# Array tiles for the query side of a sketched-attention kernel: four 32-row tiles, 64x64 tiles, and x^T without transposes

## The chip, the cores and the metric

One core of one Trainium2 chip. The metric is the device time of one execution in microseconds (us), median of several. The profile is a recording of one execution; its span runs from the first to the last instruction. In the executions that were both recorded and timed, the time is about 1.8 us longer than the span (338.94 against 337.1, 340.63 against 338.8), so I compare times with times and spans with spans. The recorded execution of the kernel before (span 363.5) is none of those timed: by the same 1.8 us it took about 365.3 us.

Engines in the profile: PE is TensorE (matmuls), PEld its weight loads, DVE is VectorE, ACT is ScalarE, POOL is GpSimd, SP is SyncE. L272 is line 272 of the file of the kernel before; the lines shift between kernels.

## The reference

Two blocks in a row, in float32:

```python
# q, k, v: [4, 4, 1088, 32]; S1, S2: [8, 32]
def phi(x):
    a = np.einsum('rd,bhsd->bhsr', S1, x)
    b = np.einsum('rd,bhsd->bhsr', S2, x)
    return np.einsum('bhsi,bhsj->bhsij', a, b).reshape(*x.shape[:-1], 64)
q_p, k_p = phi(q), phi(k)
kv = np.einsum('bhsf,bhsd->bhfd', k_p, v)
z = np.sum(k_p, axis=2)
num = np.einsum('bhsf,bhfd->bhsd', q_p, kv)
den = np.einsum('bhsf,bhf->bhs', q_p, z)[..., None] + 1e-06
x = (num / den)            # heads side by side: [4352, 128]
h = x @ w_in               # [128, 2048]
g = 0.5 * h * (1.0 + erf(h / sqrt(2)))
out = g @ w_out            # [2048, 128]
```

S1, S2, w_in and w_out arrive as float64 and are rounded to float32 on the chip. That rounding works on the bits and is done by VectorE, in eight instructions for each of eight weight quarters.

## The kernel before

The tokens are cut into nine chunks: eight of 512 tokens and a remainder of 256. For each chunk the MLP runs 16 steps of one hidden matmul (w_in, then gelu on ScalarE) and one output matmul (w_out), and the attention work for the next chunk is woven between the steps. `bufs` counts the PSUM banks (8 together, in both kernels): three for hidden, one for output, three "work" banks, one for keys.

```python
    hps = ctx.enter_context(tc.tile_pool(name="hps", bufs=3, space=PSUM))
    ops = ctx.enter_context(tc.tile_pool(name="ops", bufs=1, space=PSUM))
    wps = ctx.enter_context(tc.tile_pool(name="wps", bufs=3, space=PSUM))
    kvps = ctx.enter_context(tc.tile_pool(name="kvps", bufs=1, space=PSUM))
# ... cut: loads, constants, keys ...
        def expand(i, hp):           # factor i (0: S1, 1: S2) of one half of the rows
            rows = slice(hp * 64, hp * 64 + 64)
            ps = work_bank()
            nc.tensor.matmul(ps[:, :W], lhsT=Srep[i][rows].rearrange("p g f -> p (g f)"),
                             rhs=T["qT"][rows, :W], start=True, stop=True)
            if i == 0:
                T["A", hp] = att.tile([128, CW], FP, name="A_sb")
                nc.scalar.copy(out=T["A", hp][:, :W], in_=ps[:, :W])
            else:
                T["qp", hp] = att.tile([128, CW], FP, name="q_pT")
                nc.vector.tensor_mul(out=T["qp", hp][:, :W], in0=T["A", hp][:, :W], in1=ps[:, :W])

        def num_over_den(hp):        # tokens on partitions; 33 columns a head: numerator and denominator
            ps = work_bank()
            for i in range(nt):
                for (r0, r1, b) in owners[i]:
                    nc.tensor.matmul(ps[r0:r1, i * 2 * C:(i + 1) * 2 * C],
                                     lhsT=T["qp", hp][:, i * 128 + r0:i * 128 + r1],
                                     rhs=kv_of(b, i, hp), start=True, stop=True)
            # ... cut: views ...
            nc.vector.tensor_scalar(out=den[:, :2 * nt], in0=nd[:, :, D], scalar1=1e-6, scalar2=None, op0=AX.add)
            nc.vector.reciprocal(out=den[:, :2 * nt], in_=den[:, :2 * nt])
            nc.vector.tensor_mul(out=x_of(T["x"], hp), ...)   # cut: operands

        def x_transposes():          # back to [channel, token]
            ps = work_bank()
            for i in range(nt):
                nc.tensor.transpose(ps[:, i * 128:(i + 1) * 128], in_=T["x"][:, i, :], identity=ident)
            xT[n] = att.tile([128, CW], FP, name="xT")
            nc.vector.tensor_copy(out=xT[n][:, :W], in_=ps[:, :W])
# ... cut: the MLP; the woven stages are spread evenly over the 15 first steps:
            for f in woven[fi * len(woven) // (NF - 1):(fi + 1) * len(woven) // (NF - 1)]:
                f()
```

Of the kernel before, what the change touches and what calls it, by code (L numbers as in the profile page):

```python
# [8 lines left out]
FP = mybir.dt.float32  # L9
# [7 lines left out]
def kernel(  # L17
# [11 lines left out]
    """Sketched attention into x^T, chunk by chunk, then gelu(x @ w_in) @ w_out on each chunk.  # L29

    Tokens of a batch lie as (p j): partition p holds J tokens in a row. The last REM tokens of each batch
    are kept apart, those of two batches in one tile. All arithmetic is float32; inputs that come as float64
    come as raw bits and are rounded to float32 on chip.
    """
# [23 lines left out]
    hps = ctx.enter_context(tc.tile_pool(name="hps", bufs=3, space=PSUM))  # L58
    ops = ctx.enter_context(tc.tile_pool(name="ops", bufs=1, space=PSUM))
    wps = ctx.enter_context(tc.tile_pool(name="wps", bufs=3, space=PSUM))  # L60
# [25 lines left out]
    def landing(dst, wide):  # L86
        """Where a parameter is loaded to: its own tile, or one of 64-bit words that is rounded into it."""
        if wide:
            raw[dst.name] = big.tile([dst.shape[0], dst.shape[1], 2], U32, name=f"raw_{dst.name}")
            return raw[dst.name].rearrange("p n two -> p (n two)")  # L90
        return dst

    def words(a):
        """A parameter in DRAM in 4-byte elements, and how many of them make one number."""
# [12 lines left out]
    def round_bits(dst):  # L107
        """float64 bits to the nearest float32: mantissa as an integer times a power of two with the sign."""
# [11 lines left out]
        # exponents from 2^-127 (nought) to 2^128 (infinity)  # L120
# [24 lines left out]
    ident = big.tile([128, 128], FP, name="ident")  # L145
    mask4 = big.tile([128, H], FP, name="mask4")
    mask2 = big.tile([128, 2], FP, name="mask2")
    kv_dup = [big.tile([128, H, 2 * C], FP, name=f"kv_dup{b}") for b in range(B)]
    kv_pair = [big.tile([128, NP, 2 * C], FP, name=f"kv_pair{b}") for b in range(B)]
    make_identity(nc, ident)  # L150
    nc.gpsimd.memset(mask4, 0.0)
    nc.gpsimd.memset(mask2, 0.0)
    for h in range(H):
        nc.gpsimd.memset(mask4[h * D:(h + 1) * D, h:h + 1], 1.0)
        nc.gpsimd.memset(mask2[h * D:(h + 1) * D, h % 2:h % 2 + 1], 1.0)
    for t in kv_dup + kv_pair:
        nc.gpsimd.memset(t, 0.0)
# [3 lines left out]
    wide = [big.tile([128, R, R], FP, name=f"wide{i}") for i in range(2)]  # L161
    Srep = [big.tile([128, 2, F], FP, name=f"Srep{i}") for i in range(2)]
# [6 lines left out]
    for i in range(2):  # L169
        src = sT[:, 0:R, None] if i == 0 else sT[:, None, R:2 * R]  # L170
        nc.vector.tensor_copy(out=wide[i], in_=src.broadcast_to([128, R, R]))
        nc.vector.tensor_mul(out=Srep[i],
                             in0=wide[i].rearrange("p i j -> p (i j)")[:, None, :].broadcast_to([128, 2, F]),
                             in1=mask2[:, :, None].broadcast_to([128, 2, F]))

# [4 lines left out]
    def key_stages(b):  # L180
# [18 lines left out]
        def features(n, pair=None):  # L199
# [11 lines left out]
            for i in range(n):  # L211
                # group i is head i with its groups over j, or else the one group over the heads
# [22 lines left out]
        def finish():  # L235
# [3 lines left out]
            for j in range(2):  # L239
                src = kv3[j * F:(j + 1) * F, :, j * C:(j + 1) * C]  # L240
                for i in range(2):
                    nc.vector.tensor_copy(out=kv_dup[b][i * F:(i + 1) * F, j::2, i * C:(i + 1) * C], in_=src)  # L242
                nc.vector.tensor_copy(out=kv_pair[b][j * F:(j + 1) * F, :, j * C:(j + 1) * C], in_=src)
# [11 lines left out]
    xT = {}  # L255

    def query_stages(n, srcs, owners, kv_of, x_of):
# [170 lines left out]
```

## Time and profile before

| | before |
|---|---|
| time, median | 363.39 us (363.19 to 364.63, the first 3 runs) |
| span of the profile | 363.5 us |
| TensorE, VectorE, ScalarE busy | 95%, 29%, 26% of the span |
| first hidden matmul of chunk 0 | 37.4 us |
| a full chunk without keys, with keys | 35.7, about 43 us |

The profile is read in three steps, which the prediction shows with its lines: the page's first parts tell which engine fills the span; stretches cut at each chunk's first hidden matmul tell in which stage that holds; and in TensorE's timeline the distance between the starts of neighbours prices one inserted piece. Matmul ends are modelled and overlap (an MLP line in the timeline of the kernel before lasts 1.02 us and its like starts 0.86 us after it), so durations of TensorE lines are not added up. One float32 matmul of 512 columns is two records there (the passes): 256 lie under the 128 output matmuls of the full chunks.

### The profile page before, as it was taken

The page shows a single profiled execution, that of the slowest core. Times are in us where ns is not written, and L with a number is a line of the kernel's source. Part 1 is how long each engine was busy: PE and PEld are TensorE (multiplying, and loading weights), DVE is VectorE, ACT ScalarE, POOL GpSimd, SP SyncE. Part 2 cuts the span into 40 slices and gives each one's busy share as a digit, 9 for nine tenths or more (in the row PEclk, how much of TensorE's full clock was granted, in tenths as well). Part 3 has the DMA queues.
Part 4 walks back from the last instruction along what each step waited for, and adds up shares of the span by engine and source line. Part 5 has one row for each costly group of instructions (what it writes and reads, how often), then busy time and mean ns, then how long its engine had stood idle before and what let it go on. Part 6 is the DMA issues. An engine that isn't in the chain of part 4 may idle for free.

```text
span 363.5 us, 3051 instructions
## 1 busy us (share of the span) xinstructions
PE 345.7 (95%) x1141; PEld 178.2 (49%) x1141; DVE 103.9 (29%) x254; ACT 96.1 (26%) x173; POOL 8.4 (2%) x34
## 2 busy tenths in 40 slices
PE   1888999999999999999999999999999999999993
PEld 0875456354345663453355653543454345444582
DVE  3357796922011422230112230320122011101100
ACT  1001221323323223133223213233223322332331
POOL 4002001000000000000000000000000000000000
PEclk9999999999999999999999999999999999999997
DMA  5999100000000000000000000000000000000000
GB/s 146 327 361 348 21 0 0 2 0 29 1 2 0 29 0 2 1 0 29 0 2 0 29 0 2 0 30 0 2 0 29 0 0 2 29 0 0 0 32 14
DMA packets 13854, 13.31 MB, mean 37 GB/s; under 512 B 3856, under 2 KB 12304, under 8 KB 13840
## 3 DMA queue, kind: packets, MB, share of 16 engines
q1 hardware_dynamic: 13840, 13.13, 11.2%
q8 instruction: 9, 0.15, 0.2%
q14 instruction: 5, 0.04, 0.0%
HBM read 10.90 MB, written 2.23 MB: 36 GB/s over the span
## 4 chain that ended last, share of the span: by engine, by line
PE 92%; DVE 4%; DMA 1%; issue 1%; SPq 0%; ACT 0%; DVEq 0%
PE o_ps L343 34%; PE h_ps L334 32%; PE w_ps L272 8%; PE kv_ps L225 6%; PE w_ps L285 4%; PE w_ps L202 3%; PE w_ps L354 1%; PE w_ps L301 1%; PE w_ps L265 1%; DMA raw_SR<-in_S_dram 1%; PE w_ps L195 1%; DVE kv_dup L242 0%; DVE bits_m L118 0%; DVE k_p L213 0%; DVE bits_e L121 0%
## 5 line engine op out<-in xcount | busy, mean ns | idle before, releaser
L343 PE MATMUL o_ps<-g,w_out 128*128 128x512 f32 (+1 forms) x288 | 144.2, 585 | 0.4 <-DVE w_out L124 0.4
L334 PE MATMUL h_ps<-xT,w_in 128*128 128x512 f32 (+1 forms) x288 | 142.3, 579 | 0.6 <-DVE xT L303 0.6
L337 ACT ACTIVATE g<-h_ps 128x512 f32<-128x512 f32 (+1 forms) x144 | 82.6, 574 | 220.1 <-PE h_ps L334 220.1
L334 PEld LDWEIGHTS h_ps<-xT,w_in 128*128 128x128 f32 x288 | 54.2, 193 | 59.0 <-issue 56.5
L343 PEld LDWEIGHTS o_ps<-g,w_out 128*128 128x128 f32 x288 | 48.3, 190 | 43.9 <-issue 23.1
L279 DVE TENSOR_TENSOR q_pT<-A_sb,w_ps 128x512 f32<-128x512 f32 (+1 forms) x18 | 11.8, 658 | 95.1 <-PE w_ps L272 81.0
L272 PE MATMUL w_ps<-qT,Srep 64*128 64x512 f32 (+1 forms) x72 | 37.7, 668 | 0.0
L225 PEld LDWEIGHTS kv_ps<-v_aug,k_p 128*128 128x128 f32 x128 | 19.7, 226 | 8.0 <-issue 5.8
L272 PEld LDWEIGHTS w_ps<-qT,Srep 64*128 64x128 f32 x72 | 10.9, 200 | 24.8 <-issue 21.2
L285 PEld LDWEIGHTS w_ps<-kv_dup,q_pT 128*128 128x128 f32 x128 | 18.2, 209 | 8.7 <-issue 8.0
L225 PE MATMUL kv_ps<-v_aug,k_p 128*128 128x66 f32 x128 | 19.8, 307 | 1.3 <-DVE k_p L213 1.3
L285 PE MATMUL w_ps<-kv_dup,q_pT 128*128 128x66 f32 x128 | 17.7, 288 | 0.5 <-DVE q_pT L279 0.5
L292 DVE TENSOR_SCALAR den<-w_ps 128x8 f32<-128x8 f32 (+1 forms) x18 | 3.0, 166 | 48.6 <-PE w_ps L285 48.6
L213 DVE TENSOR_TENSOR k_p<-a_t,w_ps 128x256 f32<-128x256 f32 x32 | 11.3, 415 | 13.0 <-ACT a_t L206 13.0
L276 ACT COPY A_sb<-w_ps 128x512 f32<-128x512 f32 (+1 forms) x18 | 9.9, 563 | 12.4 <-PE w_ps L272 12.4
L267 DVE COPY qT<-w_ps 128x512 f32<-128x512 f32 (+1 forms) x9 | 6.0, 662 | 24.0 <-PE w_ps L265 23.9
L202 PEld LDWEIGHTS w_ps<-S,kT 128*128 128x128 f32 x68 | 10.6, 228 | 4.4 <-DVE kT L197 2.5
L202 PE MATMUL w_ps<-S,kT 128*128 128x64 f32 x68 | 11.0, 310 | 1.4 <-DVE kT L197 1.4
L197 DVE COPY kT<-w_ps 128x512 f32<-128x512 f32 (+1 forms) x10 | 6.1, 608 | 21.6 <-PE w_ps L195 21.6
L347 DVE COPY o_sb<-o_ps 128x512 f32<-128x512 f32 (+1 forms) x9 | 6.0, 662 | 17.6 <-PE o_ps L343 17.6
L206 ACT COPY a_t<-w_ps 128x128 f32<-128x128 f32 (+1 forms) x10 | 2.5, 249 | 27.2 <-PE w_ps L202 27.2
L303 DVE COPY xT<-w_ps 128x512 f32<-128x512 f32 (+1 forms) x9 | 6.0, 662 | 8.6 <-PE w_ps L301 8.6
(63 smaller groups left out, 121.4 us busy)
## 6 DMA issues: line engine op xcount, KB each, us to landing
k<-in_k_dram SPq DMA_DIRECT2D x4, 512.0 KB, 9.3
v<-in_v_dram SPq DMA_DIRECT2D x4, 512.0 KB, 9.7
q<-in_q_dram SPq DMA_DIRECT2D x4, 512.0 KB, 9.7
raw_w_in<-in_moe_w_in_dram SPq DMA_DIRECT2D x4, 512.0 KB, 7.2
raw_w_out<-in_moe_w_out_dram SPq DMA_DIRECT2D x4, 512.0 KB, 8.2
out_dram<-oT SPq DMA_DIRECT2D x8, 256.0 KB, 2.0
k_rem<-in_k_dram SPq DMA_DIRECT2D x4, 32.0 KB, 4.1
v_rem<-in_v_dram SPq DMA_DIRECT2D x4, 32.0 KB, 2.6
```

The source lines that it names most:

```text
L197: nc.vector.tensor_copy(out=T["kT"][:, :n * 128], in_=ps[:, :n * 128])
L202: nc.tensor.matmul(ps[:, i * 64:(i + 1) * 64], lhsT=T["kT"][:, i * 128:(i + 1) * 128], rhs=S12.rearrange("p h r -> p (h r)"), start=True, ...
L213: nc.vector.tensor_mul(out=k_p[:, :, i] if pair is None else k_p[:, 0], in0=a[:, i * H:(i + 1) * H, :, None].broadcast_to([128, H, R, R]), ...
L225: nc.tensor.matmul(T["kv"][:, hp * 2 * C:(hp + 1) * 2 * C], lhsT=lhs[:, hp * 128:(hp + 1) * 128], rhs=rhs[:, 2 * hp:2 * hp + 2, :], start= ...
L267: nc.vector.tensor_copy(out=T["qT"][:, :W], in_=ps[:, :W])
L272: nc.tensor.matmul(ps[:, :W], lhsT=Srep[i][rows].rearrange("p g f -> p (g f)"), rhs=T["qT"][rows, :W], start=True, stop=True)
L276: nc.scalar.copy(out=T["A", hp][:, :W], in_=ps[:, :W])
L279: nc.vector.tensor_mul(out=T["qp", hp][:, :W], in0=T["A", hp][:, :W], in1=ps[:, :W])
L285: nc.tensor.matmul(ps[r0:r1, i * 2 * C:(i + 1) * 2 * C], lhsT=T["qp", hp][:, i * 128 + r0:i * 128 + r1], rhs=kv_of(b, i, hp), start=True, ...
L334: nc.tensor.matmul(ps[:, :W], lhsT=w_tile(w_in_sb, fi), rhs=xT[n][:, :W], start=True, stop=True)
L337: nc.scalar.activation(out=g_of[n, fi][:, :W], in_=ps[:, :W], func=ACT.Gelu)
L343: nc.tensor.matmul(o_of[n][:, :W], lhsT=w_tile(w_out_sb, fi), rhs=g_of.pop((n, fi))[:, :W], start=(fi == 0), stop=(fi == NF - 1))
```

## The change

The intent is to take TensorE work out of the query side. A chunk's q^T has 128 rows, four groups of 32. Before, four 64-row matmuls made the two factors of the features. After, four 32-row matmuls, each on its own 32 rows and in its own bank, give both factors. The numerator is then formed with features as the contraction and *channels* on the output partitions, in four 64x64 tiles; the key sum z is repeated 32 times in the weights, so that the denominator comes out repeated on partitions, and x^T needs no transposes. The price is PSUM (two hidden banks and four work banks in place of three and three) and wider work on VectorE and ScalarE: the reciprocal is now 128x512 and not 128x8.

```diff
-    hps = ctx.enter_context(tc.tile_pool(name="hps", bufs=3, space=PSUM))
+    hps = ctx.enter_context(tc.tile_pool(name="hps", bufs=2, space=PSUM))
-    wps = ctx.enter_context(tc.tile_pool(name="wps", bufs=3, space=PSUM))
+    wps = ctx.enter_context(tc.tile_pool(name="wps", bufs=4, space=PSUM))
 ... cut: masks and zeroed key tiles go; kz holds kv and the repeated z of each batch ...
-        def expand(i, hp): ...            (shown above)
+        def expand():
+            banks = [work_bank() for g in range(4)]
+            for g in range(4):
+                rows = slice(g * D, (g + 1) * D)
+                nc.tensor.matmul(banks[g][:, :W], lhsT=Srep[rows].rearrange("p a i j -> p (a i j)"),
+                                 rhs=T["qT"][rows, :W], start=True, stop=True)
+            qp = att.tile([128, NP, CW], FP, name="q_pT")
+            T["qp"] = qp
+            for g in range(4):
+                A = att.tile([128, CW], FP, name="A_sb")
+                nc.scalar.copy(out=A[F:, :W], in_=banks[g][:F, :W])
 ... cut: the remainder's form ...
+                for r in range(2):
+                    nc.vector.tensor_mul(out=qp[r * F:(r + 1) * F, :, g * 128:(g + 1) * 128],
+                                         in0=a3[:, r::2, :], in1=b3[:, r::2, :])
-        def num_over_den(hp): ...         (shown above)
-        def x_transposes(): ...           (shown above)
+        def num_over_den():
+            banks = [work_bank() for r in range(2)]
+            for (c0, c1, b) in owners:
+                for c in range(NP):
+                    for r in range(2):
+                        nc.tensor.matmul(banks[r][c * F:(c + 1) * F, c0:c1], lhsT=kz[b][r * F:(r + 1) * F, c, :],
+                                         rhs=T["qp"][r * F:(r + 1) * F, c, c0:c1], start=True, stop=True)
+            den = att.tile([128, CW], FP, name="den")
+            for h in range(H):
+                c, r = h // 2, h % 2
+                at = c * F + (1 - r) * D
+                nc.scalar.activation(out=den[h * D:(h + 1) * D, :W], in_=banks[r][at:at + D, :W],
+                                     func=ACT.Copy, bias=1e-6)
+            nc.vector.reciprocal(out=den[:, :W], in_=den[:, :W])
+            xT[n] = att.tile([128, CW], FP, name="xT")
+            for h in range(H):
+                rows = slice(h * D, (h + 1) * D)
+                nc.vector.tensor_mul(out=xT[n][rows, :W], in0=banks[h % 2][rows, :W], in1=den[rows, :W])
 ... cut ...
-            for f in woven[fi * len(woven) // (NF - 1):(fi + 1) * len(woven) // (NF - 1)]:
+                    for at, f in zip((1, 3, 6), chunk_queries(n + 1)):
+                        slots[at].append(f)      # transposes, expansion, numerator at steps 1, 3, 6; keys from 7
```

More of the change, by code (lines that the diff above doesn't have):

```diff
@@ L146 @@
     mask4 = big.tile([128, H], FP, name="mask4")
-    mask2 = big.tile([128, 2], FP, name="mask2")
-    kv_dup = [big.tile([128, H, 2 * C], FP, name=f"kv_dup{b}") for b in range(B)]
-    kv_pair = [big.tile([128, NP, 2 * C], FP, name=f"kv_pair{b}") for b in range(B)]
+    kz = [big.tile([128, NP, 2 * D], FP, name=f"kz{b}") for b in range(B)]
     make_identity(nc, ident)
     nc.gpsimd.memset(mask4, 0.0)
-    nc.gpsimd.memset(mask2, 0.0)
     for h in range(H):
         nc.gpsimd.memset(mask4[h * D:(h + 1) * D, h:h + 1], 1.0)
-        nc.gpsimd.memset(mask2[h * D:(h + 1) * D, h % 2:h % 2 + 1], 1.0)
-    for t in kv_dup + kv_pair:
-        nc.gpsimd.memset(t, 0.0)
     sT = big.tile([128, 2 * R], FP, name="sT")
     S12 = big.tile([128, H, 2 * R], FP, name="S12")
-    wide = [big.tile([128, R, R], FP, name=f"wide{i}") for i in range(2)]
-    Srep = [big.tile([128, 2, F], FP, name=f"Srep{i}") for i in range(2)]
+    Srep = big.tile([128, 2, R, R], FP, name="Srep")
     sT_ps = work_bank()
@@ L170 @@
         src = sT[:, 0:R, None] if i == 0 else sT[:, None, R:2 * R]
-        nc.vector.tensor_copy(out=wide[i], in_=src.broadcast_to([128, R, R]))
-        nc.vector.tensor_mul(out=Srep[i],
-                             in0=wide[i].rearrange("p i j -> p (i j)")[:, None, :].broadcast_to([128, 2, F]),
-                             in1=mask2[:, :, None].broadcast_to([128, 2, F]))
+        nc.vector.tensor_copy(out=Srep[:, i], in_=src.broadcast_to([128, R, R]))
     v_rem_aug = big.tile([128, B // 2, H, C], FP, name="v_rem_aug")
@@ L239, in finish @@
             for j in range(2):
-                src = kv3[j * F:(j + 1) * F, :, j * C:(j + 1) * C]
-                for i in range(2):
-                    nc.vector.tensor_copy(out=kv_dup[b][i * F:(i + 1) * F, j::2, i * C:(i + 1) * C], in_=src)
-                nc.vector.tensor_copy(out=kv_pair[b][j * F:(j + 1) * F, :, j * C:(j + 1) * C], in_=src)
+                rows = slice(j * F, (j + 1) * F)
+                nc.vector.tensor_copy(out=kz[b][rows, :, j * D:(j + 1) * D], in_=kv3[rows, :, j * C:j * C + D])
+                nc.vector.tensor_copy(out=kz[b][rows, :, (1 - j) * D:(2 - j) * D],
+                                      in_=kv3[rows, :, j * C + D:(j + 1) * C].broadcast_to([F, NP, D]))
         stages = [widen_v]
@@ L255, with query_stages @@
     xT = {}
-    def query_stages(n, srcs, owners, kv_of, x_of):
+    def query_stages(n, srcs, by_head, owners):
         nt = len(srcs)
@@ L267, in transposes @@
             nc.vector.tensor_copy(out=T["qT"][:, :W], in_=ps[:, :W])
-        def expand(i, hp):
-            rows = slice(hp * 64, hp * 64 + 64)
-            ps = work_bank()
-            nc.tensor.matmul(ps[:, :W], lhsT=Srep[i][rows].rearrange("p g f -> p (g f)"),
-                             rhs=T["qT"][rows, :W], start=True, stop=True)
-            if i == 0:
-                T["A", hp] = att.tile([128, CW], FP, name="A_sb")
-                nc.scalar.copy(out=T["A", hp][:, :W], in_=ps[:, :W])
-            else:
-                T["qp", hp] = att.tile([128, CW], FP, name="q_pT")
-                nc.vector.tensor_mul(out=T["qp", hp][:, :W], in0=T["A", hp][:, :W], in1=ps[:, :W])
@@ L281, in num_over_den @@
-        def num_over_den(hp):
-            ps = work_bank()
-            for i in range(nt):
-                for (r0, r1, b) in owners[i]:
-                    nc.tensor.matmul(ps[r0:r1, i * 2 * C:(i + 1) * 2 * C],
-                                     lhsT=T["qp", hp][:, i * 128 + r0:i * 128 + r1],
-                                     rhs=kv_of(b, i, hp), start=True, stop=True)
-            if hp == 0:
-                T["x"] = att.tile([128, JC, d_model], FP, name="x_sb")
-            nd = ps[:, :nt * 2 * C].rearrange("p (g c) -> p g c", c=C)
-            den = att.tile([128, 2 * JC], FP, name="den")
-            nc.vector.tensor_scalar(out=den[:, :2 * nt], in0=nd[:, :, D], scalar1=1e-6, scalar2=None, op0=AX.add)
-            nc.vector.reciprocal(out=den[:, :2 * nt], in_=den[:, :2 * nt])
-            nc.vector.tensor_mul(
-                out=x_of(T["x"], hp), in0=nd[:, :, 0:D].rearrange("p (n h) d -> p n h d", h=2),
-                in1=den[:, :2 * nt].rearrange("p (n h) -> p n h", h=2)[:, :, :, None].broadcast_to([128, nt, 2, D]))
@@ L298, in x_transposes @@
-        def x_transposes():
-            ps = work_bank()
-            for i in range(nt):
-                nc.tensor.transpose(ps[:, i * 128:(i + 1) * 128], in_=T["x"][:, i, :], identity=ident)
+        def expand():
[9 more added lines that the diff above has]
+                nc.scalar.copy(out=A[F:, :W], in_=banks[g][:F, :W])
+                if by_head:
+                    half = slice(g % 2 * F, (g % 2 + 1) * F)
+                    nc.vector.tensor_mul(out=qp[half, g // 2, :W], in0=A[F:, :W], in1=banks[g][F:, :W])
+                    continue
+                a3, b3 = (t[F:, :W].rearrange("f (h p) -> f h p", h=H) for t in (A, banks[g]))
+                for r in range(2):
+                    nc.vector.tensor_mul(out=qp[r * F:(r + 1) * F, :, g * 128:(g + 1) * 128],
+                                         in0=a3[:, r::2, :], in1=b3[:, r::2, :])
@@ L302, in x_transposes @@
             xT[n] = att.tile([128, CW], FP, name="xT")
-            nc.vector.tensor_copy(out=xT[n][:, :W], in_=ps[:, :W])
-        return ([transposes] + [lambda i=i, hp=hp: expand(i, hp) for i in range(2) for hp in range(NP)]
-                + [lambda hp=hp: num_over_den(hp) for hp in range(NP)] + [x_transposes])
+            for h in range(H):
+                rows = slice(h * D, (h + 1) * D)
+                nc.vector.tensor_mul(out=xT[n][rows, :W], in0=banks[h % 2][rows, :W], in1=den[rows, :W])
@@ L308, in chunk_queries @@
+        return [transposes, expand, num_over_den]
     def chunk_queries(n):
@@ L312, in chunk_queries @@
                 n, [main["q", b][:, h, c * JC:(c + 1) * JC, :].rearrange("p j d -> p (j d)") for h in range(H)],
-                [[(0, 128, b)]] * H,
-                lambda bb, h, jp: kv_dup[bb][:, h, :],
-                lambda x, jp: x[:, 2 * jp:2 * jp + 2, :].rearrange("p j (h d) -> p h j d", h=H))
-        return query_stages(
-            n, [rem["q"][:, i, :, :].rearrange("p h d -> p (h d)") for i in range(B // 2)],
-            [[(0, REM, 2 * i), (REM, 2 * REM, 2 * i + 1)] for i in range(B // 2)],
-            lambda bb, i, hp: kv_pair[bb][:, hp, :],
-            lambda x, hp: x[:, :B // 2, hp * 64:(hp + 1) * 64].rearrange("p n (h d) -> p n h d", h=2))
+                False, [(0, CW, b)])
+        return query_stages(n, [rem["q"][:, i, :, :].rearrange("p h d -> p (h d)") for i in range(B // 2)],
+                            True, [(b * REM, (b + 1) * REM, b) for b in range(B)])
     NCHUNK = B * NCH + 1
@@ L383 @@
             if fi == 0:
-                woven = []
+                slots = [[] for _ in range(NF)]
+                if n + 1 < NCHUNK:
+                    for at, f in zip((1, 3, 6), chunk_queries(n + 1)):
+                        slots[at].append(f)
                 if n % NCH == 0 and n // NCH + 1 < B:
-                    woven += key_stages(n // NCH + 1)
-                if n + 1 < NCHUNK:
-                    woven += chunk_queries(n + 1)
-            for f in woven[fi * len(woven) // (NF - 1):(fi + 1) * len(woven) // (NF - 1)]:
+                    keys = key_stages(n // NCH + 1)
+                    for i, f in enumerate(keys):
+                        slots[7 + i * (NF - 7) // len(keys)].append(f)
+            for f in slots[fi]:
                 f()
```

## The prediction

> **What bounds the kernel now.** I read the page first (busy shares, slices, chain of waits), then the instruction groups with shapes kept apart, then the busy time of each engine chunk by chunk, then the timeline of TensorE. From the page:
>
> ```profile
> PE 345.7 (95%) x1141; PEld 178.2 (49%) x1141; DVE 103.9 (29%) x254; ACT 96.1 (26%) x173; POOL 8.4 (2%) x34
> PE   1888999999999999999999999999999999999993
> ...
> PE 92%; DVE 4%; DMA 1%; issue 1%; SPq 0%; ACT 0%; DVEq 0%
> ...
> L272 PE MATMUL w_ps<-qT,Srep 64*128 64x512 f32 (+1 forms) x72 | 37.7, 668 | 0.0
> ```
>
> TensorE is busy 95% of the span, without a hole from the third slice to the last but one, and 92% of the chain that ended last is TensorE work. The query expansion (L272) alone is 37.7 us. The other engines sit below 30%. So TensorE time that is removed shortens the kernel unless another engine takes the bound. The windows view, cut where each chunk's first hidden-layer matmul starts (the first number is the stretch), shows where that is in doubt:
>
> ```profile
> 37.38:79.19 41.80, 41.43 (x151) 22.28 (x152) 32.18 (x77) 11.16 (x20) 1.10 (x2) 1.00 0.01 1
> 79.19:114.90 35.72, 35.72 (x101) 15.88 (x100) 5.73 (x12) 10.72 (x18) 0.00 (x0) 1.00 0.02 8
> 114.90:158.16 43.26, 43.26 (x164) 22.53 (x163) 11.91 (x30) 11.34 (x22) 0.00 (x0) 1.00 0.02 7
> ```
>
> The columns after the length are busy time of TensorE, weight loads, VectorE and ScalarE. From chunk 1 on TensorE is full and VectorE nearly idle (5.73 of 35.72 us). In chunk 0 VectorE is busy 32.18 of 41.80 us, because it rounds the float64 weights then. A chunk with keys woven in costs 43.26 − 35.72 = 7.5 us more.
>
> The TensorE timeline gives the price of each part. A line with x2 is one float32 matmul in two passes, so starts are to be subtracted, not durations:
>
> ```profile
> 164.33 1.02 PE L334 MATMUL h_ps<-xT,w_in 128*128 128x512 f32 x2
> 165.28 1.12 PE L272 MATMUL w_ps<-qT,Srep 64*128 64x512 f32 x2
> 166.33 1.12 PE L343 MATMUL o_ps<-g,w_out 128*128 128x512 f32 x2
> 167.30 1.02 PE L334 MATMUL h_ps<-xT,w_in 128*128 128x512 f32 x2
> ...
> 183.06 1.02 PE L334 MATMUL h_ps<-xT,w_in 128*128 128x512 f32 x2
> 183.92 1.00 PE L285 MATMUL w_ps<-kv_dup,q_pT 128*128 128x66 f32 x8
> 184.76 1.08 PE L343 MATMUL o_ps<-g,w_out 128*128 128x512 f32 x2
> 185.67 1.02 PE L334 MATMUL h_ps<-xT,w_in 128*128 128x512 f32 x2
> ...
> 190.86 0.60 PE L301 MATMUL w_ps<-ident,x_sb 128*128 128x128 f32 x4
> 191.29 1.02 PE L343 MATMUL o_ps<-g,w_out 128*128 128x512 f32 x2
> ```
>
> An MLP matmul beside its like takes 0.858 us start to start (five of them from 156.44 to 160.73 in this view). From 164.33 to 167.30 are 2.97 us for two MLP matmuls and one 64-row expansion, so the expansion costs 2.97 − 1.716 = **1.25 us**[...]. One group of numerator matmuls (L285) costs 185.67 − 183.06 − 1.716 = **0.89 us**, and the x transposes (L301) **0.43 us**. A full chunk has four expansions (5.02), two groups (1.78), x transposes (0.43), q transposes (0.44), output transposes (0.58) and 32 MLP matmuls (27.46): 35.71 against the measured 35.72, so nothing is left unexplained.
>
> [...]
>
> ```profile
> 66.78 1.98 PE L272 MATMUL w_ps<-qT,Srep 64*128 64x512 f32 x6
> ...
> 68.70 1.13 PE L334 MATMUL h_ps<-xT,w_in 128*128 128x512 f32 x2
> ...
> 332.02 0.45 PE L285 MATMUL w_ps<-kv_pair,q_pT 128*64 128x66 f32 x8
> 332.40 1.12 PE L343 MATMUL o_ps<-g,w_out 128*128 128x512 f32 x2
> ```
>
> Three expansions issued together (two row halves, then one) took 1.92 us, [...]about two matmul times, not three; and eight 64-column passes took 0.38 us, 0.05 each. Four at once isn't in this trace. [...]the trace gives
>
> ```profile
> L293 DVE RECIPROCAL den<-den 128x8 f32<-128x8 f32 x16 | 3.2, 202 | 0.5
> L293 DVE RECIPROCAL den<-den 128x4 f32<-128x4 f32 x2 | 0.4, 178 | 0.1
> ```
>
> that is (202 − 178)/4 = 6 ns an element, so for the new 128x512 reciprocal an estimate of 3.2 us[...].
>
> **The change part by part, a full chunk.**
> (1) Expansion: four 64-row matmuls in four places become four 32-row matmuls side by side, each giving both factors, in four banks. If they overlap: 0.86 + 0.40 and a few hundredths = 1.28 instead of 5.02, saving 3.74.
> (2) Numerator and denominator: sixteen narrow-output passes become four 64x64 tiles of N=512, 1.28 instead of 1.78 if all four overlap, saving 0.50. If only two do, 2.1: a loss of 0.36.
> (3) x transposes go: 0.43 saved.
> Together **4.67 us per chunk**: 35.7 becomes about 31.0.
> (4) ScalarE: four A copies instead of two and four denominator copies more, at 0.59 us each like A_sb now: 10.7 becomes about 14 of 31 us. VectorE: eight 64x256 products (0.34 start to start, like k_p), the reciprocal (3.2), four 32x512 products (0.6 start to start) in place of two products, den, x and the xT copy: 5.7 becomes about 11.5 us. Both stay hidden from chunk 1 on. In chain: after the expansion, copies and products take some 3.6 us (two A buffers, so VectorE paces), and the numerator comes three steps (5.2 us) later; reciprocal and products end some 8 us after that, with nine steps left.
> (5) One hidden bank less (two for three): the hidden matmul two steps on needs the gelu of now, 0.6 us in a step of 1.72. Hidden.
>
> **The start** goes the other way. In the prologue all of this is in series. Now the first x^T is ready at 37.3. After, the expansion starts at about 25.6 as now, but TensorE is still slow here (passes take twice as long): 2 us, then 3.4 for the products, 2 for the numerator, 2 for the copies, 3.2 for the reciprocal and 2.5 for the products: about 41.1, so **+3.8 us**. In chunk 0 VectorE then needs about 22 us for the remaining weight rounding, 9 for the query chunk and 5 for keys, 36 us beside TensorE's 39.6; it blocks TensorE where a weight isn't rounded in time. I put that at 1.5 us, and chunk 0's own saving at 3.0 (its expansions were partly paired already).
>
> **Sum.** Chunks 1 to 6: 6 × 4.67 = 28.0. Chunk 7 carries the remainder's query (256 wide): now 4.7, after 1.7, 3.0 saved. Chunk 0: 3.0 − 1.5. Start: −3.8. Net 28.7: 363.4 − 28.7 = 334.7. Unforeseen waits tend to add; I say **336 us**.
>
> **Rivals.** (a) VectorE or ScalarE becomes the bound: in chunks 1 to 7 against it are 11.5 and 14 busy us in 31; for it, in chunk 0, are 32 of 41.8 us already. At most some 6 us more, about 341. (b) The 64x64 tiles overlap only in pairs[...]: seven times 0.9[...]. (c) New waits replace the removed work: the expansion needs all four work banks free at once, and bursts of four ScalarE copies hold up gelus. The slack above speaks against it; 1 us a chunk makes 344. (d) In the key chunks the reciprocal stands ahead of the key copy in VectorE's order, and TensorE[...] waits for it: up to 1 or 2 us in two chunks. (e) No concurrency at all: expansion 3.8 and numerator 3.8 per chunk, about 355 to 360. The paired passes at 66.78 speak against that.
>
> **Range and chances.** If all goes as hoped and the start costs nothing, 330; two of (a) to (d) together give 346. Range 329 to 346. Faster by over 2% needs less than 356.1, missed only under (e) or something like it: 0.95; within 2% 0.04, slower 0.01.
>
> **What the profile after should show.** Chunk spacing of about 31.0 us (38.5 with keys); eight expansion passes ahead of the next MLP matmul in about 1.1 us; the same for the numerator; no transposes of x; reciprocals of 3.2 us; the first hidden matmul near 41 us; TensorE still about 95% busy. It would be wrong if the expansion passes start one after another, if chunk spacing in the middle is over 33 us with ACT or DVE named as releasers, or if chunk 0 takes over 46 us.

The text is as recorded; passages that no trace or run of this case shows are cut out and marked. No term of the main sum is among them: it came to 363.4 − 28.7 = 334.7 us, and to 336 with the allowance. That four tiles overlap was the assumption; the trace before shows only the three expansions in 1.92 us and the eight 64-column passes in 0.38 us. The 0.40 us in "0.86 + 0.40" is what a 64-row matmul between MLP matmuls costs in the trace before beyond an MLP matmul: 1.25 − 0.858. Its cause was not shown. Rival (b) had a second case, of 0.3 us a chunk, which no trace shows; with it the rival came to about 344 us, with the 0.9 us a chunk alone to 342. "Twice as long" at the start is 0.85 us from pass to pass of the first hidden matmuls (38.40, 39.25 us), where later it is 0.43.

## The result

| | before | changed |
|---|---|---|
| time, median | 364.01 us (363.19 to 364.80, 4 runs) | 339.00 us (338.94 to 339.04, 4 runs) |
| span of the profile | 363.5 us | 337.1 us |
| TensorE, VectorE, ScalarE busy | 95%, 29%, 26% | 92%, 45%, 37% |
| first hidden matmul of chunk 0 | 37.4 us | 41.9 us |
| chunks 0 and 1 together | 77.5 us | 73.2 us |
| a later full chunk without keys | 35.7 us | 31.0 us |

The ratio is 0.9304, 95% interval 0.9281 to 0.9326: faster. The ratios here and below are not quite the ratios of the medians (339.00 over 364.01 is 0.931). The output is correct.

The page of the changed kernel, the same parts as shown of before:

```profile
PE 308.6 (92%) x1059; PEld 154.9 (46%) x1059; DVE 150.8 (45%) x276; ACT 125.4 (37%) x227; POOL 6.0 (2%) x21
PE   1895099799999999999999999999999999999993
...
PE 84%; DVE 13%; DMA 1%; issue 0%; SPq 0%; ACT 0%; DVEq 0%
```

TensorE has 37 us less busy time, but its row of slices now has holes: the fourth and fifth digits, 5 and 0, are the start, where TensorE waits, and the 7 is a hole in chunk 0. The chain has 13% of VectorE where before it had 4%. So something was given back at the start and in chunk 0. The stretches by chunk (length, then busy time of TensorE, weight loads, VectorE, ScalarE, GpSimd, then the granted TensorE clock):

```profile
41.93:80.12 38.19, 36.00 (x114) 16.83 (x115) 35.91 (x73) 13.96 (x25) 0.00 (x0) 0.96 0.00 0
80.12:115.11 34.99, 34.99 (x112) 16.13 (x110) 12.88 (x22) 14.69 (x25) 1.10 (x2) 1.00 0.02 8
115.11:153.62 38.51, 38.51 (x153) 20.00 (x152) 17.02 (x32) 14.71 (x27) 0.00 (x0) 1.00 0.02 7
153.62:184.59 30.97, 30.97 (x89) 13.21 (x88) 11.56 (x16) 14.11 (x24) 0.00 (x0) 1.00 0.02 9
```

From chunk 2 on TensorE is full again, and chunks 2 to 6 are 4.5 to 4.8 us shorter than before. In chunk 0 VectorE is busy 35.91 of 38.19 us and TensorE isn't full. Chunk 1 is long only because matmuls of chunk 0 slipped into it (112 passes against 89 in a clean chunk), so I take the two together. The timeline of TensorE in a later stretch shows the two new groups (x8 is eight passes, four float32 matmuls):

```profile
90.31 1.02 PE L325 MATMUL h_ps<-xT,w_in 128*128 128x512 f32 x2
91.26 1.14 PE L267 MATMUL w_ps<-qT,Srep 32*128 32x512 f32 x8
92.33 1.13 PE L334 MATMUL o_ps<-g,w_out 128*128 128x512 f32 x2
...
96.73 1.02 PE L325 MATMUL h_ps<-xT,w_in 128*128 128x512 f32 x2
97.68 1.09 PE L288 MATMUL w_ps<-q_pT,kz 64*64 64x512 f32 x8
98.70 1.13 PE L334 MATMUL o_ps<-g,w_out 128*128 128x512 f32 x2
```

Eight expansion passes stand between 91.26 and 92.33, that is 1.07 us, where before *one* 64-row matmul of two passes took 1.05. The eight passes of the 64x64 tiles take 1.02 us. So in both forms four matmuls side by side take about as long as one 64-row matmul alone.

**The start.** TensorE's timeline until the first hidden matmul, then VectorE's in its second half:

```profile
24.46 2.09 PE L267 MATMUL w_ps<-qT,Srep 32*128 32x512 f32 x8
30.33 2.52 PE L288 MATMUL w_ps<-q_pT,kz 64*64 64x512 f32 x8 [3.78 <-DVE q_pT L280]
...
41.93 1.22 PE L325 MATMUL h_ps<-xT,w_in 128*128 128x512 f32 x1 [8.03 <-DVE xT L300]
```

```profile
35.44 3.34 DVE L296 RECIPROCAL den<-den 128x512 f32<-128x512 f32 x1
...
39.09 2.79 DVE L300 TENSOR_TENSOR xT<-w_ps,den 32x512 f32<-32x512 f32 x4
```

The brackets give TensorE's idle time and who ended it: 3.78 us for the feature products and 8.03 us for x^T, in which ScalarE copies the denominators, then VectorE takes the reciprocal (3.34 us) and the four products (2.79 us). The expansion itself begins 1.2 us sooner than before, yet x^T is ready 4.5 us later. The same two points of the kernel before:

```profile
25.66 4.88 PE L272 MATMUL w_ps<-qT,Srep 64*128 64x512 f32 x8
...
37.38 1.22 PE L334 MATMUL h_ps<-xT,w_in 128*128 128x512 f32 x1 [0.57 <-DVE xT L303]
```

**Chunk 0.** VectorE and TensorE around the hole (VectorE lines first):

```profile
62.46 3.35 DVE L296 RECIPROCAL den<-den 128x512 f32<-128x512 f32 x1
...
65.73 0.64 DVE L124 SCALAR_TENSOR_TENSOR w_out<-bits_m,bits_e 128x512 f32<-128x512 f32 x1
...
66.42 1.12 PE L334 MATMUL o_ps<-g,w_out 128*128 128x512 f32 x2 [1.97 <-DVE w_out L124]
```

TensorE waits 1.97 us for a quarter of w_out whose last rounding instruction stands behind the reciprocal. Stretches cut around the hole (clock in the third field from the right):

```profile
60.00:66.40 6.40, 4.45 (x14) 1.89 (x12) 6.37 (x10) 1.79 (x3) 0.00 (x0) 1.00 0.00 0
...
68.00:71.40 3.40, 3.40 (x10) 1.66 (x9) 3.34 (x7) 0.60 (x1) 0.00 (x0) 0.56 0.00 0
```

After the hole the granted clock falls to about half for 3.4 us (by its records to 0.50, from 67.6 to 71.0 us). At that clock TensorE does some 1.7 us less work in this time (0.50 x 3.4), but most of it would have been lost without the fall too. The lines that follow (TensorE, VectorE, then a weight load of TensorE):

```profile
67.38 1.69 PE L325 MATMUL h_ps<-xT,w_in 128*128 128x512 f32 x2
...
69.66 0.69 DVE L188 COPY kT<-w_ps 128x512 f32<-128x512 f32 x1
...
70.40 1.25 PEld L193 LDWEIGHTS w_ps<-S,kT 128*128 128x128 f32 x8 [1.20 <-DVE kT L188]
```

The key matmuls of L193 need kT, whose copy stands on VectorE behind the x^T products. At 0.858 us a matmul TensorE would have reached them at 67.38 + 1.72 = 69.10 and waited until 70.40; it reached them at 70.57. By this estimate the loss in chunk 0 is 2.0 us of waiting for w_out, 1.3 us of a second wait for VectorE, which the slow clock only covers, and about 0.4 us of the clock itself. Another execution agrees: the record gives one of the changed kernel a mean clock of 0.997, which leaves about 1 us of lost clock in its whole span, less than the 1.7 us of this fall, and its time is 339.04 us all the same.

### The profile page after: what moved, and what is told of

Read it like the earlier page. It is cut to its first block, busy times and chain, and to the rows that moved or that the text cites. A ratio compares the mean times of both kernels' runs of the same rounds, so it can differ in the third digit from the quotient of the medians. Undisturbed runs are those within 1.5% of the kernel's fastest.

```text
span 337.1 us, 2831 instructions
## 1 busy us (share of the span) xinstructions
PE 308.6 (92%) x1059; PEld 154.9 (46%) x1059; DVE 150.8 (45%) x276; ACT 125.4 (37%) x227; POOL 6.0 (2%) x21
## 4 chain that ended last, share of the span: by engine, by line
PE 84%; DVE 13%; DMA 1%; issue 0%; SPq 0%; ACT 0%; DVEq 0%
PE o_ps L334 34%; PE h_ps L325 32%; PE kv_ps L216 6%; PE w_ps L193 3%; PE w_ps L267 3%; DVE q_pT L280 2%; PE w_ps L288 2%; DVE den L296 2%; PE w_ps L345 2%; DVE bits_e L123 1%; DVE bits_m L118 1%; PE w_ps L259 1%; PE w_ps L186 1%; DMA raw_SR<-in_S_dram 1%; DVE bits_e L122 1%; DVE xT L300 1%
## 5 line engine op out<-in xcount | busy, mean ns | idle before, releaser
L334 PE MATMUL o_ps<-g,w_out 128*128 128x512 f32 (+1 forms) x288 | 142.7, 580 | 2.0 <-DVE w_out L124 2.0
L334 PEld LDWEIGHTS o_ps<-g,w_out 128*128 128x128 f32 x288 | 51.5, 191 | 55.0 <-issue 49.5
L296 DVE RECIPROCAL den<-den 128x512 f32<-128x512 f32 (+1 forms) x9 | 28.6, 3174 | 33.3 <-ACT den L294 33.3
L280 DVE TENSOR_TENSOR q_pT<-A_sb,w_ps 64x256 f32<-64x256 f32 x64 | 27.1, 424 | 18.3 <-ACT A_sb L273 17.0
L273 ACT COPY A_sb<-w_ps 64x512 f32<-64x512 f32 (+1 forms) x36 | 19.1, 553 | 17.5 <-PE w_ps L267 10.3
L300 DVE TENSOR_TENSOR xT<-w_ps,den 32x512 f32<-32x512 f32 (+1 forms) x36 | 23.6, 657 | 0.9
L294 ACT ACTIVATE den<-w_ps 32x512 f32<-32x512 f32 (+1 forms) x36 | 20.3, 565 | 6.7 <-PE w_ps L288 6.3
L288 PE MATMUL w_ps<-q_pT,kz 64*64 64x512 f32 (+1 forms) x96 | 10.8, 523 | 3.8 <-DVE q_pT L280 3.8
L193 PEld LDWEIGHTS w_ps<-S,kT 128*128 128x128 f32 x68 | 10.7, 233 | 5.6 <-DVE kT L188 4.0
L193 PE MATMUL w_ps<-S,kT 128*128 128x64 f32 x68 | 11.4, 318 | 1.3 <-DVE kT L188 1.3
L267 PE MATMUL w_ps<-qT,Srep 32*128 32x512 f32 (+1 forms) x72 | 10.8, 671 | 0.0
L347 DVE COPY oT<-w_ps 128x512 f32<-128x512 f32 (+1 forms) x9 | 6.0, 662 | 6.5 <-PE w_ps L345 6.5
```

The lines of the kernel that those rows point to most:

```text
L193: nc.tensor.matmul(ps[:, i * 64:(i + 1) * 64], lhsT=T["kT"][:, i * 128:(i + 1) * 128], rhs=S12.rearrange("p h r -> p (h r)"), start=True, ...
L267: nc.tensor.matmul(banks[g][:, :W], lhsT=Srep[rows].rearrange("p a i j -> p (a i j)"), rhs=T["qT"][rows, :W], start=True, stop=True)
L273: nc.scalar.copy(out=A[F:, :W], in_=banks[g][:F, :W])
L280: nc.vector.tensor_mul(out=qp[r * F:(r + 1) * F, :, g * 128:(g + 1) * 128], in0=a3[:, r::2, :], in1=b3[:, r::2, :])
L288: nc.tensor.matmul(banks[r][c * F:(c + 1) * F, c0:c1], lhsT=kz[b][r * F:(r + 1) * F, c, :], rhs=T["qp"][r * F:(r + 1) * F, c, c0:c1], star ...
L294: nc.scalar.activation(out=den[h * D:(h + 1) * D, :W], in_=banks[r][at:at + D, :W], func=ACT.Copy, bias=1e-6)
```

## The experiments

Theory A: the steady gain is the overlap of tiles brought together (expansion 3.7, the rest 0.9 us a chunk), and what is missing was lost to VectorE: at the start, where the wide denominator stands in series, and in chunk 0, where rounding fills VectorE. Rivals: the gain belongs to 32-row tiles as such or to the numerator; what is missing is lost to fewer hidden banks, the four-bank wait, or everywhere a little. The first four kernels split the change, e5 to e9 take VectorE work away (e6 is a control), and e10 to e12 move the woven work to other steps. "Chunks 0+1" and "later" (a full chunk without keys) are read from the trace. In the expectations of e3 and e4 clauses on the cause of the 0.40 us are cut and marked.

| run | time, us | ratio to before (95%) | start | chunks 0+1 | later |
|---|---|---|---|---|---|
| changed | 339.0 | 0.930 (0.928 to 0.933) | 41.9 | 73.2 | 31.0 |
| e1_expand_only | 339.4 | 0.931 (0.928 to 0.935) | 37.8 | 72.4 | 32.0 |
| e2_num_only | 365.0 | 1.002 (0.999 to 1.006) | 43.4 | 77.1 | 34.7 |
| e3_group_only | 341.8 | 0.939 (0.935 to 0.942) | 37.6 | 71.9 | 32.8 |
| e4_spread32 | 363.3 | 0.997 (0.994 to 1.000) | 42.2 | 76.6 | 34.7 |
| e5_after_less_rounding (wrong result) | 334.9 | 0.919 (0.915 to 0.923) | 42.2 | 69.6 | 31.0 |
| e6_before_less_rounding (wrong result) | 365.7 | 1.003 (0.999 to 1.008) | 36.4 | 77.7 | 35.7 |
| e7_copy_for_reciprocal (wrong result) | 336.3 | 0.924 (0.920 to 0.928) | 39.4 | 74.3 | 31.0 |
| e9_narrow_two | 333.5 | 0.916 (0.912 to 0.919) | 37.9 | 71.9 | 31.0 |
| e8_narrow_first | 337.4 | 0.927 (0.922 to 0.931) | 37.6 | 75.6 | 31.0 |
| e10_two_later | 332.2 | 0.910 (0.908 to 0.912) | 37.7 | 70.6 | 31.0 |
| e11_reciprocal_later | 338.9 | 0.929 (0.924 to 0.934) | 42.1 | 74.7 | 31.0 |
| e12_narrow_first_later | 336.8 | 0.924 (0.920 to 0.927) | 37.9 | 73.7 | 31.0 |

### e1_expand_only

```diff
 # from the changed kernel
-        return [transposes, expand, num_over_den]
+        return [transposes, expand] + [lambda hp=hp: num_over_den(hp) for hp in range(NP)] + [x_transposes]
 # numerator, denominator, x transposes and key tiles as before; the product of group g is one 64x512 instruction;
 # stages at steps 1, 3, 6, 7, 9
```

> Part 1 alone: the four 32-row expansions of the change, but numerator, denominator and x transposes of the kernel before. My theory: the gain is nearly all in the expansion and the loss at the start all in the wide denominator. A chunk without keys takes 35.72 - 3.74 = 31.98 us, the first hidden matmul starts at about 36.6 us (before 37.4, changed 41.9), chunk 0 does not stall on rounded weights, total about 336 us, so below the changed kernel. Rival: the gain needs both parts (the numerator's tiles carry as much); then a chunk takes over 33 us and the total is over 345.

Measured: later chunks 31.98 us, exactly the expected; start 37.8, 1.2 later than expected; TensorE stood idle for 1.7 us in chunk 0, 0.6 before a hidden matmul whose quarter of w_in had just been rounded and 1.1 for a kT copy queued behind rounding, and I had excluded such waits; time 339.4 instead of 336. The expansion carries 3.74 of the 4.75 us a chunk, and the other two parts 1.01. Over the whole kernel the other two parts bring nothing: 339.4 against 339.0, because what they save in the later chunks they lose at the start (4.1 us) and in chunks 0 and 1 (0.8 us).

### e2_num_only

```diff
 # from the changed kernel
-        return [transposes, expand, num_over_den]
+        return ([transposes] + [lambda i=i, hp=hp: expand(i, hp) for i in range(2) for hp in range(NP)]
+                + [num_over_den])
 # expand(i, hp), Srep and masks as before, with products written in the new layout; stages at steps 1, 2, 3, 4, 5, 7
```

> Parts 2 and 3 alone: the 64x64 numerator with repeated denominator and no x transposes, but the four separate 64-row expansions of before. My theory: a chunk without keys takes 35.72 - 0.93 = 34.8 us; the first hidden matmul starts at about 44 us because expansions, products, denominator copies and reciprocal stand in series; total about 365 us, so no gain at all by itself. Rival: the numerator carries its own weight, total under 360.

Measured: 34.70 us a later chunk, start 43.4, time 365.0, ratio 1.002: as the theory had it. Alone, this part changes nothing in the whole: the later chunks gain 1.0 us each, the start loses 6.0.

### e3_group_only

```diff
 # from the kernel before
+        def expand_all():
+            banks = {}
+            for i in range(2):
+                for hp in range(NP):
+                    banks[i, hp] = work_bank()
+                    nc.tensor.matmul(banks[i, hp][:, :W], lhsT=Srep[i][rows]..., rhs=T["qT"][rows, :W], ...)
+            # then the two copies and the two products as before
-        [transposes] + [lambda i=i, hp=hp: expand(i, hp) for i in range(2) for hp in range(NP)] ...
+        [transposes, expand_all] ...      # steps 1 and 3; numerators at 6 and 7, x transposes at 9; hps 2, wps 4
```

> The kernel before with nothing new but the place of its four 64-row expansions: issued together with four work banks (and two hidden banks) instead of spread over the chunk. My theory: two pairs overlap[...], so an expansion group costs 2 x 0.858 + 0.40 = 2.12 us instead of 5.02, a chunk without keys 32.8 us, total about 343 us: most of the gain is in bringing them together. Rival: only 32-row tiles overlap in steady state or grouping makes waits for banks; then a chunk is 34.5 to 35.7 us.

Measured: 32.83 us a later chunk, time 341.8. TensorE's timeline:

```profile
156.74 1.99 PE L275 MATMUL w_ps<-qT,Srep 64*128 64x512 f32 x8
158.65 1.12 PE L345 MATMUL o_ps<-g,w_out 128*128 128x512 f32 x2
```

Four 64-row matmuls in 1.91 us, the time of two MLP matmuls (1.72) and 0.2 more: two pairs. Between the MLP matmuls that start at 155.78 and 159.62 the group costs 3.84 − 1.716 = 2.12 us, as expected. So issuing the old matmuls together gives 2.89 of the 4.75 us a chunk, and 22.8 of the 25 us of the whole change, with no new layout and no loss at the start. It also has two hidden banks and four work banks, and the chunk came out as the sum of its parts, so the banks cost nothing there. Its woven stages also stand at fixed steps and no longer spread evenly; the next run has such fixed steps and the same banks without the grouping, and doesn't have the gain.

### e4_spread32

```diff
 # from the changed kernel
-        def expand():
-            banks = [work_bank() for g in range(4)]
-            for g in range(4):
+        def expand(g):
+            banks = {g: work_bank()}
 # one group a stage
-                    for at, f in zip((1, 3, 6), chunk_queries(n + 1)):
+                    for at, f in zip((1, 2, 3, 4, 5, 7), chunk_queries(n + 1)):
```

> The changed kernel with its four 32-row expansions issued one at a time in four steps, MLP matmuls between them. My theory: a 32-row matmul alone costs as much as a 64-row one, 1.25 us[...], so a chunk without keys takes 30.97 + 3.74 = 34.7 us and the total is about 366 us. Rival: a 32-row matmul is cheaper in itself (fewer rows)[...]; then a chunk stays under 33 us.

Measured: 34.70 us a later chunk, as expected; time 363.3, not 366.

```profile
172.14 1.12 PE L267 MATMUL w_ps<-qT,Srep 32*128 32x512 f32 x2
173.19 1.12 PE L335 MATMUL o_ps<-g,w_out 128*128 128x512 f32 x2
```

One 32-row matmul alone takes 1.05 us, as long as a 64-row one, and between MLP matmuls (171.19 to 174.16) it costs 2.97 − 1.716 = 1.25 us, as much too. Using fewer rows of the array saves nothing here; being next to each other saves all of the 3.7 us (34.70 against 30.97). The rival falls.

### e5_after_less_rounding and its control, e6_before_less_rounding

```diff
 # e5 from the changed kernel, e6 from the kernel before; the result is wrong on purpose
+    w_out_use = [w_out_sb[0]] * WCH
-        nc.tensor.matmul(o_of[n][:, :W], lhsT=w_tile(w_out_sb, fi), ...
+        nc.tensor.matmul(o_of[n][:, :W], lhsT=w_tile(w_out_use, fi), ...
-                round_bits(w_out_sb[i])
+                if i == 0:
+                    round_bits(w_out_sb[i])
```

> Wrong result on purpose: the changed kernel, but only the first quarter of w_out is rounded and used for all four, which takes about 10.7 us (24 instructions) from VectorE in chunk 0. My theory: what chunks 0 and 1 lose (73.2 us together against 38.8 + 31.0 = 69.8 by TensorE's work) comes from VectorE being full in chunk 0, so that TensorE waits for rounded weights and then runs slow for a while. Then they take about 69.8 us, the start stays at 41.9 and the total is about 335.6 us. Rival: it is the two hidden banks or the four-bank wait; then chunks 0 and 1 stay at 73 us and the total at 339.

> Wrong result on purpose: the same cut of rounding in the kernel before, as a control. My theory: there VectorE has slack in chunk 0 (one wait of 0.5 us for w_out), so chunks 0 and 1 go from 77.5 to about 77.0 us and the total by 0.5 to 1 us, to about 363.5. Rival: rounding costs the same in both kernels; then about 3.4 us are saved here too.

Measured: e5 has 38.58 + 30.97 = 69.6 us for chunks 0 and 1, no hole in either, and 334.9 us in all. e6 has 77.7 us, no gain; its times (364.5 to 366.0) aren't told apart from those of the kernel before in this call (363.1 to 365.7). So 3.6 us of the change's expected gain were lost because the wide query work and the rounding share VectorE in chunk 0. The line of chunk 0 in e5:

```profile
42.22:80.80 38.58, 38.58 (x136) 19.32 (x137) 27.10 (x54) 14.58 (x26) 1.10 (x2) 0.92 0.00 0
```

TensorE is full at 38.58 us once VectorE has 27.10 us of work instead of 35.91.

### e7_copy_for_reciprocal

```diff
 # from the changed kernel; the result is wrong on purpose
-            nc.vector.reciprocal(out=den[:, :W], in_=den[:, :W])
+            nc.vector.tensor_copy(out=den[:, :W], in_=den[:, :W])
```

> Wrong result on purpose: the changed kernel with the nine wide reciprocals (3.35 us each) replaced by copies of the same size (about 0.4). My theory: in chunks 1 to 7 they are hidden, so only the start (41.9 to 39.0) and chunks 0 and 1 (73.2 to about 70.5) gain: total about 333.5 us. Rival: VectorE paces the steady chunks too; then each chunk gains and the total falls below 325 us.

Measured: start 39.4 (39.0 expected) and later chunks 31.0: the reciprocal costs 2.6 us at the start (the copy in its place takes 0.43 us, not 3.35) and nothing in steady state. But chunks 0 and 1 took 74.3 us, not 70.5: a miss. The kernel's text differs in one line, but TensorE's order came out another: matmuls of the keys moved ahead and waited 3.1 us for a copy that stood behind the x^T products on VectorE; the clock fell after that hole too (a hidden matmul at 67.48 took 1.70 us start to start, not 0.86; the mean over chunk 0 is 0.96). So this run doesn't measure what the reciprocal costs in chunk 0.

### e9_narrow_two and e8_narrow_first

```diff
 # from the changed kernel: the form of before (narrow denominator) for the first two chunks, in e8 for the first only
+        if n < 2:
+            return [transposes, expand] + [lambda hp=hp: num_narrow(hp) for hp in range(NP)] + [x_transposes]
         return [transposes, expand, num_over_den]
```

> A version meant to beat both: the changed kernel, with the numerator, denominator and x transposes of before for the first two chunks only, where they stand at the start or where VectorE is full; correct result. My theory: start at about 37.8 us and chunk 0 at 40.4 us as in the run with the expansion alone, chunk 1 at about 31.0 us, the rest as in the changed kernel (222.0 us from chunk 2 on): span about 331.2, time about 333 us, some 6 us below the changed kernel. Rival: the second form costs more elsewhere (both kinds of keys, other order): 336 us or more.

> The changed kernel with the numerator, denominator and x transposes of before for the first chunk only. My theory: the wide form costs some 4 us at the start and nothing else depends on it there: start at 37.9 us instead of 41.9, chunks 0 and 1 together still about 73 us, time about 335 us. Rival: the earlier start finds VectorE less far with the rounded weights, and chunk 0 gives the 4 us back: time about 338 us.

Measured: e9 takes 333.5 us with a correct result, as expected. Its chunk 0 (40.9 us) still has one wait of 1.9 us for w_out. e8 takes 337.4 us: the start is 4.3 us earlier, but chunks 0 and 1 take 75.6 us, so more than half of that is given back. The rival was nearer: with x^T ready sooner, VectorE is less far with the rounding, two holes of 2.3 and 2.65 us, both for w_out, open in TensorE, and the clock falls (to 0.59 in the stretch from 54.5 to 58.2 us) after the first, not after the second.

### e10_two_later

```diff
 # from e9
-   zip((1, 3, 6) if n + 1 >= 2 else (1, 3, 6, 7, 9), chunk_queries(n + 1))
+   zip((1, 3, 6) if n + 1 >= 2 else (1, 5, 9, 10, 12), chunk_queries(n + 1))
```

> The run with the narrow form in the first two chunks, but in chunk 0 the next chunk's expansion is issued two steps later and its numerator two to three steps later, so that VectorE's rounding for w_out comes first. My theory: the 2.1 us wait for w_out in chunk 0 goes; chunk 0 takes about 39 us instead of 40.9, time about 332 us. Rival: VectorE is simply full and the wait moves elsewhere: 333 to 334 us.

Measured: 332.2 us, ratio 0.910, the best of all and correct. Chunk 0:

```profile
37.67:77.32 39.65, 39.65 (x148) 21.60 (x149) 33.36 (x79) 12.30 (x22) 1.10 (x2) 1.00 0.00 1
```

TensorE is busy for all of 39.65 us and the clock doesn't fall after the start; no wait is left in chunk 0.

### e11_reciprocal_later and e12_narrow_first_later

```diff
 # from the changed kernel (e11) and from e8 (e12): in chunk 0 keys from step 4, the next numerator at 11
-                    for at, f in zip((1, 3, 6), chunk_queries(n + 1)):
+                    for at, f in zip((1, 3, 6) if n else (1, 3, 11), chunk_queries(n + 1)):
-                        slots[7 + i * (NF - 7) // len(keys)].append(f)
+                        slots[(7 + i * (NF - 7) // len(keys)) if n else (4 + i * (NF - 4) // len(keys))].append(f)
```

> The changed kernel, all its work kept, but in chunk 0 the numerator and reciprocal of the next chunk come at step 11 instead of 6 and the keys from step 4 on, so that all rounding stands ahead of the reciprocal. My theory: it is the 3.35 us reciprocal ahead of a rounded quarter of w_out that makes TensorE wait (and its clock drop after it), so place is enough: chunks 0 and 1 go from 73.2 to about 70.5 us, time about 336.5 us. Rival: VectorE's 36 us in chunk 0 are the bound whatever the order: still 73 us, 339 us.

> Both cures together: the narrow form in the first chunk only, and in chunk 0 the numerator and reciprocal of the next at step 11. My theory: the two losses are separate and add: start at 37.9, chunks 0 and 1 about 70.5 us, time about 332.5 us, 6.5 us below the changed kernel. Rival: with the earlier start VectorE has less time for rounding and the second cure works less: 334 us or more.

Measured: both theories fell. In e11 all rounding now precedes the reciprocal, but the wait only moved: TensorE waits 1.7 us for key features on VectorE, the granted clock is 0.50 from 65.0 to 70.5 us, and chunks 0 and 1 take 74.7 us. Chunk 0 of e11:

```profile
42.08:84.34 42.26, 40.26 (x120) 19.19 (x121) 36.57 (x74) 14.54 (x26) 0.00 (x0) 0.92 0.00 0
```

e12 has a hole of 2.4 us for w_out and one of 1.4 us for the next chunk's x^T, which the later numerator made late, and 73.7 us. With 35 to 37 us of VectorE work in chunk 0 neither the order of the change nor this one avoids the waits. With 33.1 and 33.4 us (e9, e10) the order decides: e9 has one wait, e10 none. I can't say that no order would do it with 36 us, only that moving the reciprocal doesn't.

**Still open.** The executions of e7, e8, e11 and e12 lie in groups some 2 to 4 us apart (337.2, 337.4 and 340.5, 340.6 in e11), while the changed kernel's four agree within 0.1 us. A hole that sometimes makes the clock fall (1.97 us in the changed kernel) and sometimes doesn't (1.92 us in e9) would do that, but only one execution of each was recorded, so this is argued, not shown. The mean clocks speak for it in part: in e11 the two slow executions have 0.988, as the recorded one with its fall, and a fast one has 0.996, but the other fast one has 0.983. In e12 the recorded execution had a fall and took 335.5 us, and one at 0.996 took 335.8, so there the fall made no difference. What makes the two groups of the kernel before was not looked into.

## Why the prediction was right

The range (329 to 346) holds 339.0 us, and the sum of steps can be checked term by term, in spans:

| step | predicted | measured |
|---|---|---|
| full chunk without keys | −4.67 | −4.74 to −4.75 |
| of that the expansion (e1) | −3.74 | −3.74 |
| of that numerator and x transposes (changed against e1) | −0.93 | −1.01 |
| chunks 2 and 4, with keys | −4.67 | −4.75, −4.55 |
| chunk 7, with the remainder's query | −3.0 | −3.02 |
| the start | +3.8 | +4.55 |
| chunks 0 and 1 together | −1.5 − 4.67 = −6.2 | −4.3 |
| all | −28.7 | −26.3 |

1. **The bound and the price of an insertion** were right. The distance between starts, not the durations, gave 1.25 us for one expansion, and e4 confirms that it is the same for 32 rows.
2. **Four tiles side by side** was the step that the trace before couldn't show. It was right: 1.07 us for eight passes. Rivals (b) and (e) fell. Rival (e) was also priced wrongly: its 3.8 + 3.8 us a chunk are more than the 5.0 + 1.8 + 0.4 of before, so without any overlap the change would have been slower than before, not 355 to 360 us.
3. **Steady VectorE and ScalarE** were right: 11.56 and 14.11 us busy in a chunk against 11.5 and 14 predicted; e7 shows that the reciprocal is hidden there. Rivals (c) and (d) fell: chunks 2 and 4 show no wait to speak of.
4. **The start** was right in kind, but its sum has a slip: the terms as written add up to 40.7 us, not 41.1. Measured are 41.9. The expansion began 1.1 us sooner than assumed, and what follows was longer: feature products 3.8 instead of 3.4 us, numerator 2.5 instead of 2, denominator copies 2.4 instead of 2, reciprocal 3.34 instead of 3.2, products 2.8 instead of 2.5, and 0.5 us of gaps, a rounding instruction ahead of the products among them.
5. **Chunk 0** was the term that was mis-sized: I put the waits for rounded weights at 1.5 us, and the two chunks lost 3.6 us against e5. 2.0 us of it are the wait for w_out. The rest is, by the estimate under "Chunk 0", mostly a second wait, for the keys' kT behind the x^T products, which I hadn't counted at all; the granted clock adds about 0.4 us. It is rival (a), in the stage where I expected it. TensorE came out 92% busy, not about 95%.

The 336 us already had 1.3 us added to the sum for unforeseen waits; the unforeseen came to about 2.4 us in the span. In time the sum, 334.7, was 4.3 us short: the other 1.9 us come from taking terms of a trace of about 365.3 us off a median time of 363.4. The range held with both; the allowance of 1.3 us was too small for the two together.

## What to carry to other kernels

Bring matmuls that use part of the array's rows next to each other before rewriting them: e3 moved four old 64-row matmuls together and got 22.8 of the 25 us. When a change takes work from the full engine and gives it to an idle one, ask stage by stage whether that engine is idle there: here it was idle most of the time in the later chunks, and the start and the first chunk gave back 8 us. A second form for those places (e10) got most of it back.

## What the traces show of the hardware

- Four 32-row matmuls side by side took 1.07 us start to start where four MLP matmuls take 3.43 (4 x 0.858): 3.2x, with the wider distances of the neighbours' starts before and after it (0.95 and 0.96 us, not 0.858) left out. Alone, such a matmul takes 1.05 us (e4).
- A 64-row or 32-row matmul between MLP matmuls costs 0.40 us beyond the 0.86 us of one MLP matmul (1.25 us in the kernel before and in e4). Four 64-row matmuls next to each other cost it once: 2.12 us in e3, which is 2 x 0.858 + 0.40. The cause of the 0.40 us was not shown.
- A hole of 2.0 us idle in the changed kernel was followed by 3.4 us at a granted clock of about half (0.56 in that stretch), and in e11 a hole of 1.7 us by 0.50, while the clock stayed at 1.00 after a hole of 1.9 us in e9 and did not fall after one of 2.65 us in e8 (the earlier fall, to 0.59 for 3.7 us and 0.97 for 5.5, is all of chunk 0's mean of 0.96). So the length of the hole alone doesn't tell.
- The clock is missing at the start of both traces: the first clock record of the kernel before comes at 42.3 us, that of the changed kernel at 47.1. For the kernel before the field reads 1.00 from 37.4 to 41.0 us, where passes take 0.85 us and not 0.43. There the start distances tell more than the clock field.
- The reciprocal of 128x512 takes 3.35 us, 6.5 ns an element; the narrow one (128x8, 128x4) gave 6 ns an element before.
